# Seven half products for the first pair too, neighbouring chunks' products joined, and another order of the list

## The chip, the cores and the metric

The kernel runs on one core of one Trainium2 chip. Its time is the device time of one launch in microseconds; the profile is of one execution and splits it by engine: PE multiplies matrices (PEld loads its weights), DVE, ACT and POOL work elementwise, SP issues most DMAs. All data are float32.

## The reference

A gated recurrence over the sequence per head, with a complex gate, and then a low-rank mixer. Batch 4, heads 8, sequence 768, head size 48, so the model width is 384 and the mixer's inner width 1536.

```python
def _attn_ref(q, k, v, a_re, a_im):
    mag = np.sqrt(a_re * a_re + a_im * a_im)
    scale = np.minimum(mag, 0.999) / (mag + 1e-06)
    a_re_n, a_im_n = (a_re * scale, a_im * scale)
    ...
    for t in range(S):
        ar, ai = (a_re_n[:, :, t, :, None], a_im_n[:, :, t, :, None])
        new_re = ar * S_re - ai * S_im
        new_im = ar * S_im + ai * S_re
        kv = np.einsum('bhd,bhe->bhde', k[:, :, t], v[:, :, t])
        S_re, S_im = (new_re + kv, new_im)
        y[:, :, t] = np.einsum('bhd,bhde->bhe', q[:, :, t], S_re)

def _moe_ref(x, U, V, w_ch1, w_ch2):
    xt = x.transpose(0, 2, 1)
    h = xt @ U @ V
    u = x + h.transpose(0, 2, 1)
    ch = np.maximum(u @ w_ch1, 0.0) @ w_ch2
    return (u + ch).astype(np.float32)
```

`U` is 768x32, `V` 32x768, `w_ch1` 384x1536 (called w1 below), `w_ch2` 1536x384 (w2).

## The kernel before

**Chunks and pairs.** The sequence is cut into chunks of 128 positions, 6 in a batch and 24 in all, i = 0 to 23. A chunk is worked on in halves of 64. Two neighbouring chunks make a pair of the mixer, m = 0 to 11, three pairs in a batch.

**A chunk.** The gates' logarithms and angles are summed along the sequence by products with a triangle (L777, L782, L842); ACT makes exponentials (es) and sines and cosines (cs) of them, for which it loads another table each time (L463). The running angle is handed from one chunk group to the next by a carry: one small DMA on POOL's queue (L828) from the tile F into the next gate tile, which DVE reads at L836 and L837 before PE can form the next prefix (L842). DVE multiplies q and k by es and cs (L469), and the result is turned, by PE for the first six chunks and by a transposing DMA after that.

`chain(i)` then records the products of a chunk. `products` (L956) are keys by queries, with the array split 112x64; DVE masks them into AT (`copy_predicated`, L959). `state` (L976) is keys by values on tiles of 64x48, into two banks; DVE adds them to the running state (GM and G, L472, and G times its decay T, L469). `inside` (L1005) is AT by values on 64x64 and `before` (L1013) the state by queries on 112x64, both into the same two banks y, which ACT copies into xo, the attention's output (L1022, L1024). A matmul in float32 is two records in the trace.

**The mixer.** For a batch, `rank` (L1048) forms U-transposed by x; ACT copies it to r (L1054); `spread` (L1071) multiplies it by V, and DVE adds that to xo (`mixed`), which is now u. `turned` (L1087) transposes u into uT. The first layer of pair 0 is made ahead of the mixing (`up`, L1102) and then corrected by V times the tile `more` (`corrected`, L1142, `more` copied by ACT at L1128); pair 1 takes `up` after the mixing; pairs 2 to 11 take `up_fewer` (L1214), fifteen block products. ACT and DVE apply the relu and sums into h, for pair 0 into the tile `extra`.

**The second layer.** Pair 0 takes `down(cc)` (L1303): 12 products of 128x384 for each of its two chunks, over w2 in steps of two blocks, so that each step needs only the part of w2 that it reads. Later pairs take `down_two()` (L1346): the pair's 2x2 block product by seven half products, each six matmuls of 128x192, of sums of h's blocks (`sums`, DVE L1338) and differences of w2's blocks (`w2s`, made once by DVE at L652 from the whole of w2, in the tile `stage`). The first pair that uses it also turns one quarter of w2 into a difference in place (L1416). DVE adds the results onto xo (L472), and `leave` sends them out. w1 and w2 come from memory in pieces through `stage`, and ACT and DVE split each piece into a high and a low part (L466, L616, L620, L624, L472) during the first 120 us.

**What sets the order.** Every step is recorded with its engine, what it reads, writes and takes over, and ORDER is the list of record numbers in which the steps are issued, for all engines; each engine runs its share in that order, so an instruction that waits holds all behind it on its engine. SPARE and WARM put idle matmuls of the identity (fillers, L1506 and L1513) ahead of the record numbers that they name; SPARE counts matmuls of 128 columns, WARM lists column counts in units of 128. Of PSUM, five banks go round among the prefix, state, output and transpose steps, two hold the mixer's results (`up`, `few`, `down`), one the keys by queries.

## Time and profile before

| | us |
|---|---|
| median of 3 runs (lowest, highest) | 530.83 (529.35, 532.6) |
| profiled execution | 529.77 |
| its span | 528.0 |
| first matmul starts after | 7.7 |
| PE busy | 509.3 (6670 records) |
| DVE busy | 414.5 |
| ACT busy | 346.0 |
| POOL busy | 31.6 |

A line of the profile names an engine, the line of the kernel, the operation and the tiles out<-in by the program's names without buffer numbers, with a shape of partitions x elements. In a timeline it begins with the start and the duration in us; in a group `x` is the number of records, followed by total us and mean ns, and by the idle time of the engine just ahead of them. `[2.10 <-ACT more L1128]` is idle time of the engine ahead of an instruction, and what ended it.

### The profile page before, as it was taken

How to read it: one execution, taken by the hardware profiler on the slowest of the kernel's cores; microseconds unless marked ns; L12 is line 12 of the kernel's file. 1: busy time of each engine (PE TensorE's matmuls, PEld its weight loads, DVE VectorE, ACT ScalarE, POOL GpSimd, SP SyncE). 2: the span in 40 equal slices, each digit the busy share in tenths (PEclk: the TensorE clock that was granted, in tenths of full speed). 3: DMA queues.
4: the chain of work that ended last, by engine and by line, in shares of the span. 5: the costliest groups of instructions: out<-in, count | busy, mean ns of one | idle time of the engine just before them, and what ended most of it. 6: DMA issues, size and time to landing. Idle time of an engine off the chain costs nothing.

```text
span 528.0 us, 15692 instructions
## 1 busy us (share of the span) xinstructions
PE 509.3 (96%) x6670; PEld 460.3 (87%) x6670; DVE 414.5 (79%) x787; ACT 346.0 (66%) x555; POOL 31.6 (6%) x61
## 2 busy tenths in 40 slices
PE   4999999899999999999999999999999999999996
PEld 2777887666998997999999989999999989999996
DVE  4779897799989987898798797878796575958452
ACT  8899998998869978978896768843543313131100
POOL 1000000001010000101011000110000000000110
PEclk9999999999999999999999999999999999999998
DMA  9959958479999998999899958999897543333101
GB/s 226 173 115 270 209 115 191 140 138 217 197 215 244 216 215 145 204 217 202 205 198 227 210 144 175 170 242 229 192 217 178 108 90 61 76 60 61 39 32 35
DMA packets 280670, 87.06 MB, mean 165 GB/s; under 512 B 271288, under 2 KB 272784, under 8 KB 280592
## 3 DMA queue, kind: packets, MB, share of 16 engines
q1 hardware_dynamic: 278384, 81.63, 76.0%
q0 software_dynamic: 2208, 4.35, 2.4%
q8 instruction: 54, 0.88, 0.7%
q14 instruction: 24, 0.20, 0.1%
HBM read 43.03 MB, written 23.63 MB: 126 GB/s over the span
## 4 chain that ended last, share of the span: by engine, by line
PE 88%; ACT 5%; DMA 3%; DVE 2%; issue 1%; SPq 0%; ACTq 0%
PE down L1346 25%; PE few L1214 14%; PE bank L1214 11%; PE up L1102 6%; PE inner L956 4%; PE bank L1013 4%; PE bank L976 4%; PE down L1303 3%; PE bank L1005 2%; DMA gate<-F 2%; PE bank L1071 2%; PE bank L1087 2%; ACT gate L466 1%; PE bank L777 1%; PE bank L782 1%; PE bank L842 1%
## 5 line engine op out<-in xcount | busy, mean ns | idle before, releaser
L466 ACT ACTIVATE gate<-gate 128x768 f32<-128x768 f32 (+2 forms) x85 | 86.1, 1018 | 25.8 <-DMA gate<-in_a_im_dram 14.7
L1346 PE MATMUL down<-w,h 128*128 128x192 f32 x396 | 70.4, 328 | 0.0
L466 ACT ACTIVATE QK<-QKC 128x768 uint16<-128x768 uint16 (+1 forms) x72 | 58.5, 848 | 13.1 <-DVE QKC L469 7.9
L1346 PEld LDWEIGHTS down<-w,h 128*128 128x128 f32 x396 | 64.6, 190 | 1.2 <-issue 0.8
L469 DVE TENSOR_TENSOR QKC<-qk,cs 128x768 f32<-128x768 f32 x48 | 44.9, 952 | 1.0 <-ACT cs L466 0.6
L472 DVE TENSOR_TENSOR xo<-down,xo 128x192 f32<-128x192 f32 (+1 forms) x79 | 29.9, 385 | 14.3 <-PE down L1346 14.1
L1222 ACT COPY h<-few 128x512 f32<-128x512 f32 x35 | 20.2, 583 | 27.8 <-PE few L1214 27.6
L1222 ACT COPY h<-bank 128x512 f32<-128x512 f32 x25 | 14.3, 588 | 36.0 <-PE bank L1214 31.0
L1346 PE MATMUL down<-stage 128*128 128x192 f32 x198 | 37.2, 328 | 0.0
L1102 PE MATMUL up<-uT,w 128*128 128x256 f32 x144 | 33.8, 383 | 0.0
L1346 PEld LDWEIGHTS down<-stage 128*128 128x128 f32 x198 | 32.5, 190 | 0.3 <-issue 0.2
L1102 PEld LDWEIGHTS up<-uT,w 128*128 128x128 f32 x144 | 26.7, 190 | 4.9 <-issue 0.6
L1290 POOL DMA_DIRECT2D out_dram<-xo x32 | 18.5, 590 | 202.9 <-DVE xo L472 164.5
L463 ACT ACT_TABLE_LOAD x22 | 28.2, 1283 | 1.1 <-PEq L1567 0.7
L828 POOL DMA_DIRECT2D gate<-F x15 | 12.0, 797 | 274.7 <-DVE stage L616 86.3
L1226 DVE CUSTOM_DVE_ANT_1 h<-few,h 128x512 f32<-128x512 f32 x31 | 21.0, 686 | 8.8 <-PE few L1214 8.1
L1214 PE MATMUL few<-extra,w 128*128 128x128 f32 x216 | 27.8, 275 | 0.0
L956 PE MATMUL inner<-QK 112*64 112x64 f32 x768 | 27.5, 224 | 0.2 <-DVE AT L959 0.2
L466 ACT ACTIVATE cs<-F 128x384 f32<-128x384 f32 x48 | 24.4, 518 | 3.9 <-DVE F L851 3.7
L956 PEld LDWEIGHTS inner<-QK 112*64 112x64 f32 x768 | 24.5, 138 | 2.4 <-issue 0.8
L1214 PEld LDWEIGHTS few<-extra,w 128*128 128x128 f32 x216 | 26.3, 192 | 0.1
L466 ACT ACTIVATE es<-bank 128x384 f32<-128x384 f32 x44 | 18.4, 502 | 9.2 <-PE bank L777 8.2
(185 smaller groups left out, 1166.8 us busy)
## 6 DMA issues: line engine op xcount, KB each, us to landing
xd<-QK SPq DMA_DIRECT2D x36, 512.0 KB
gate<-in_a_re_dram SPq DMA_DIRECT2D x48, 192.0 KB
gate<-in_a_im_dram SPq DMA_DIRECT2D x48, 192.0 KB
stage<-in_moe_w_ch_dram SPq DMA_DIRECT2D x12, 768.0 KB
qk<-in_q_dram SPq DMA_DIRECT2D x24, 192.0 KB
qk<-in_k_dram SPq DMA_DIRECT2D x24, 192.0 KB
VP<-in_v_dram SPq DMA_DIRECT2D x24, 192.0 KB
out_dram<-xo POOLq DMA_DIRECT2D x12, 192.0 KB, 4.2
```

Of the source, the lines that this page charges most:

```text
L463: ACT(1.37, rank, lambda: nc.scalar.preload_act_table_set(name), writes=[TABLE])
L466: return nc.scalar.activation(out=o, in_=i, func=f, **kw)
L469: nc.vector.tensor_tensor(out=o, in0=a, in1=b, op=OP.mult)
L472: nc.vector.tensor_tensor(out=o, in0=a, in1=b, op=OP.add)
L956: nc.tensor.matmul(out=get(*ps0)[r:r + HC, h], lhsT=k_of(h, r, HC), rhs=q_of(h, r, HC), start=True, stop=True, tile_position=(0, r))
L976: nc.tensor.matmul(out=get(*dk[r])[x:x + D, h], lhsT=get(*ks)[at, h, x // DP, 0:D], rhs=get(*VPi)[at, h], start=True, stop=True, tile_posi ...
L1013: nc.tensor.matmul(out=get(*y[u])[side(r, u), p], lhsT=q_of(h, r * HC, HC), rhs=get(*(mid_G if r else ("G", i - 1)))[:, h], start=False, s ...
L1102: nc.tensor.matmul(out=get(*ps)[:, e], lhsT=w1[:, f, (ff + e) * 128:(ff + e + 1) * 128], rhs=get(*uT)[:, f], start=(f == 0), stop=(f == KD ...
L1214: nc.tensor.matmul(out=get(*ps)[:, q], lhsT=w()[:, q * 128:(q + 1) * 128], rhs=v[0](), start=(n == 0 and q == 0), stop=True, skip_group_ch ...
L1222: ACT(c_act(n3 * CH) - 0.045, RU, lambda i=i, k=k: nc.scalar.copy(out=at(i, k), in_=get(*ps)), [ps], [o])
L1226: DVE(c_dve(n3 * CH), RU, lambda i=i, k=k: nc.vector._custom_dve(dve_ops.TENSOR_ADD_SAT, out=at(i, k), in0=get(*ps), in1=at(i, k), s0=math ...
L1346: nc.tensor.matmul(out=get(*to)[:, part], lhsT=x(j), rhs=y[:, j], start=(first and j == 0), stop=(j == KH - 1), skip_group_check=not first)
```

## The change

PLAIN goes from 1 to 0: pair 0 too takes `down_two()`. Its h is the tile `extra`; the turning of w2's quarter (L1416, after the change L1459) moves to pair 0, which now needs all of w2 and its differences. JOIN = 8: from chunk 8 on, where a chunk is not the first of its batch, its `state` products and its predecessor's `inside` are recorded as one step (`fused_x`), and its predecessor's two `before` and its own `products` as another (`fused_y`); the addition into G and the multiplication by T, the masking and the predecessor's copies to xo follow the second. These are 14 of the 24 chunks. The spread no longer names uT among what it reads; the transposes take uT over instead. ORDER, SPARE and WARM are replaced by others. Below L1040 the lines shift by 43, above it by a few: L1102 becomes L1145, L1142 L1185, L1087 L1130, L1048 L1091, L1071 L1114, L1346 L1389, L1338 L1381, L1506 L1549, L1513 L1556; L956 becomes L962, L976 L974, L1005 L998, L1013 L1006.

```diff
--- before.py
+++ after.py
@@ -29,101 +29,100 @@
 ORDER = (
...
-    5, 97, 96, 0, 1, 2, 3, 102, 99, 101, 103, 4, 104, 105, 106, 107, 98, 116, 100, 115, 117, 118, 119, 10, 154, 8, 111, 112, 16, 9, 230, 108, 231,
...
+    5, 96, 0, 1, 2, 3, 4, 99, 97, 102, 101, 103, 104, 105, 8, 98, 116, 100, 115, 117, 9, 111, 106, 107, 108, 109, 118, 119, 120, 121, 125, 126, 122,
...
 SPARE = {
-    410: 3, 447: 1,
+    413: 3, 416: 6, 430: 4, 462: 1,
 }
...
 WARM = {
-    112: (2, 1), 126: (1,), 136: (2, 2, 2, 2, 2, 2, 1), 141: (2,), 162: (2, 2, 2), 235: (2, 2, 2, 2, 1), 242: (2,), 245: (2,), 259: (2, 2, 1), 266: (1, 1, 1, 1, 1, 1, 1, 1, 1),
+    125: (4,), 136: (4, 2, 2, 2, 2, 1), 141: (2,), 162: (2, 2, 2), 187: (1,), 235: (2, 2, 2, 2, 2, 2, 2), 242: (3,), 245: (2,), 259: (1,), 266: (2, 2, 2, 2, 1),
 }
...
@@ -352,7 +351,7 @@
     KH = KF // 2
     DH = DM // 2
 
-    PLAIN = 1
+    PLAIN = 0
     NS = 5
     FEWER, SINGLE, AHEAD = 2, 3, 1
     NCH = S // CH
@@ -369,6 +368,7 @@
     PARTS = [[(n, n + 1) for n in range(GC)]] + [[g] for g in GROUPS[1:]]
     NG = len(GROUPS)
     AGAIN = range(NG)
+    JOIN = 8
 
     EARLY, SPREAD = 6, (0, 1, 2)
     SPLIT = range(3, NG)
@@ -948,51 +948,44 @@
             return get(*QK)[0:DQ, 1, h * CH + lo:h * CH + lo + n]
 
         ps0 = ("inner", i)
-        psum(ps0, "A", [128, H, HC])
+        last = c == NCH - 1
+        joined, joins = c > 0 and i >= JOIN, not last and i + 1 >= JOIN
+        G, mid_G = ("G", i), ("GM", i)
+        ks, dk = ("qkc", 2 * i + 1), [("dk", (i, r)) for r in range(2)]
+        parts_k = range(1 if last else 2)
+        y, xi = [("y", (i, r)) for r in range(2)], ("xo", i)
+        y_in = [VPi, ATi, mid_G] + ([("G", i - 1)] if c else [])
 
         def products():
             for h in range(H):
                 for r in range(0, CH, HC):
                     nc.tensor.matmul(out=get(*ps0)[r:r + HC, h], lhsT=k_of(h, r, HC), rhs=q_of(h, r, HC), start=True, stop=True,
                                      tile_position=(0, r))
-        PE(0.947, RL, products, [QK], [ps0], takes=[ATi], way=1, steps=4 * H)
-        DVE(0.17 + 0.00104 * H * HC, RL, lambda: nc.vector.copy_predicated(
-            out=get(*ATi), mask=mask.bitcast(I32).unsqueeze(1).to_broadcast([128, H, HC]), data=get(*ps0)), [ps0, ("mask", 0)], [ATi])
-
-        G, mid_G, last = ("G", i), ("GM", i), c == NCH - 1
-        ks, dk = ("qkc", 2 * i + 1), [("dk", (i, r)) for r in range(2)]
-        buffer(mid_G, "GM", 2, [DQ, H, D])
-        if not last:
-            buffer(G, "G", 2, [DQ, H, D])
-        parts_k = range(1 if last else 2)
-        for r in parts_k:
-            psum(dk[r], "Y", [128, H, D], [128, H, DP])
-
-        def state(h0):
-            for h in range(h0, h0 + HH):
+
+        def kept():
+            DVE(0.17 + 0.00104 * H * HC, RL, lambda: nc.vector.copy_predicated(
+                out=get(*ATi), mask=mask.bitcast(I32).unsqueeze(1).to_broadcast([128, H, HC]), data=get(*ps0)), [ps0, ("mask", 0)], [ATi])
+
+        def state(h0, n=HH):
+            for h in range(h0, h0 + n):
                 for r in parts_k:
                     at = slice(r * HC, (r + 1) * HC)
                     for x in (0, DP):
                         nc.tensor.matmul(out=get(*dk[r])[x:x + D, h], lhsT=get(*ks)[at, h, x // DP, 0:D], rhs=get(*VPi)[at, h],
                                          start=True, stop=True, tile_position=(r * HC, x))
-        for h0 in (0, HH):
-            PE(0.443, RR, lambda h0=h0: state(h0), [ks, VPi], [dk[r] + (h0,) for r in parts_k], way=3,
-               steps=4 * HH * len(parts_k),
-               takes=[mid_G] + ([] if last else [G]))
 
         half0, half1 = (lambda r=r: get(*dk[r])[0:DQ] for r in range(2))
-        if c:
-            DVE(c_dve(DM), RR, lambda: add(get(*mid_G), get("G", i - 1), half0()), [("G", i - 1), dk[0]], [mid_G])
-        else:
-            ACT(c_act(DM), RR, lambda: nc.scalar.copy(out=get(*mid_G), in_=half0()), [dk[0]], [mid_G])
-        if not last:
-            DVE(c_dve(DM), RR, lambda: add(get(*G), get(*mid_G), half1()), [mid_G, dk[1]], [G])
-            DVE(c_dve(DM), RR, lambda: mul(get(*G), get(*G), T_of(i)), [("T", group_of(i))], [G])
-
-        y, xi = [("y", (i, r)) for r in range(2)], ("xo", i)
-        for r in range(2):
-            psum(y[r], "Y", [128, HH, D], [128, HH, CH])
-        buffer(xi, "xo", 8, [128, DM])
+
+        def states(first):
+            if not first:
+                pass
+            elif c:
+                DVE(c_dve(DM), RR, lambda: add(get(*mid_G), get("G", i - 1), half0()), [("G", i - 1), dk[0]], [mid_G])
+            else:
+                ACT(c_act(DM), RR, lambda: nc.scalar.copy(out=get(*mid_G), in_=half0()), [dk[0]], [mid_G])
+            if not last and first != joined:
+                DVE(c_dve(DM), RR, lambda: add(get(*G), get(*mid_G), half1()), [mid_G, dk[1]], [G])
+                DVE(c_dve(DM), RR, lambda: mul(get(*G), get(*G), T_of(i)), [("T", group_of(i))], [G])
 
         def side(r, u):
             return slice((r ^ u) * HC, (r ^ u) * HC + HC)
@@ -1013,18 +1006,68 @@
                     nc.tensor.matmul(out=get(*y[u])[side(r, u), p], lhsT=q_of(h, r * HC, HC),
                                      rhs=get(*(mid_G if r else ("G", i - 1)))[:, h], start=False, stop=True,
                                      tile_position=(0, (r ^ u) * HC), skip_group_check=True)
-        PE(0.44, RR, inside, [VPi, ATi, mid_G] + ([("G", i - 1)] if c else []), y, way=3, takes=[xi], steps=4 * H)
+
+        def befores():
+            for r in range(0 if c else 1, 2):
+                before(r)
+
+        def rooms():
+            for r in range(2):
+                psum(y[r], "Y", [128, HH, D], [128, HH, CH])
+            buffer(xi, "xo", 8, [128, DM])
+
+        def halves(a):
+            return a.rearrange("p (a u d) -> p a u d", u=2, d=D)
+
+        def leaves():
+            ACT(c_act(HH * D) - 0.04, RR, lambda: nc.scalar.copy(out=halves(get(*xi))[:, :, 0], in_=get(*y[0])), [y[0]], [xi + (0,)])
+            for r in range(2):
+                ACT(c_act(HH * D) + 0.04, RR, lambda r=r: nc.scalar.copy(out=halves(get(*xi))[r * HC:(r + 1) * HC, :, 1],
+                                                                         in_=get(*y[1])[side(r, 1)]), [y[1] + (r,)], [xi + (r + 1,)])
+        b_in = [QK, mid_G] + ([("G", i - 1)] if c else [])
+        psum(ps0, "A", [128, H, HC])
+        buffer(mid_G, "GM", 2, [DQ, H, D])
+        if not last:
+            buffer(G, "G", 2, [DQ, H, D])
+        for r in parts_k:
+            psum(dk[r], "Y", [128, H, D], [128, H, DP])
+        if joined:
+            p_inside, p_in, p_y, p_befores, p_b, p_leaves, p_rooms, p_takes = pending.pop(i - 1)
+            p_rooms()
+
+            def fused_x():
+                state(0, H)
+                p_inside()
+            PE(1.3, RR, fused_x, [ks, VPi] + p_in, [dk[r] for r in parts_k] + p_y, way=3, steps=4 * H * len(parts_k) + 4 * H,
+               takes=[mid_G] + p_takes)
+            states(True)
+
+            def fused_y():
+                p_befores()
+                products()
+            PE(1.8, RR, fused_y, p_b + [QK], p_y + [ps0], takes=[ATi], way=1, steps=8 * H)
+            states(False)
+            kept()
+            p_leaves()
+        else:
+            PE(0.947, RL, products, [QK], [ps0], takes=[ATi], way=1, steps=4 * H)
+            kept()
+            for h0 in (0, HH):
+                PE(0.443, RR, lambda h0=h0: state(h0), [ks, VPi], [dk[r] + (h0,) for r in parts_k], way=3,
+                   steps=4 * HH * len(parts_k),
+                   takes=[mid_G] + ([] if last else [G]))
+            states(True)
+        if joins:
+            pending[i] = inside, y_in, y, befores, b_in, leaves, rooms, [xi]
+            return
+        rooms()
+        PE(0.44, RR, inside, y_in, y, way=3, takes=[xi], steps=4 * H)
         if c:
             PE(0.467, RR, lambda: before(0), [QK, ("G", i - 1)], [y[0] + (0,), y[1] + (0,)], way=1, steps=2 * H)
         PE(0.467, RR, lambda: before(1), [QK, mid_G], [y[0] + (1,), y[1] + (1,)], way=1, steps=2 * H)
-        def halves(a):
-            return a.rearrange("p (a u d) -> p a u d", u=2, d=D)
-        ACT(c_act(HH * D) - 0.04, RR, lambda: nc.scalar.copy(out=halves(get(*xi))[:, :, 0], in_=get(*y[0])), [y[0]], [xi + (0,)])
-        for r in range(2):
-            ACT(c_act(HH * D) + 0.04, RR, lambda r=r: nc.scalar.copy(out=halves(get(*xi))[r * HC:(r + 1) * HC, :, 1],
-                                                                     in_=get(*y[1])[side(r, 1)]), [y[1] + (r,)], [xi + (r + 1,)])
-
-
+        leaves()
+
+    pending = {}
 
     def mixer(m, ahead=False):
         i0 = m * MC
@@ -1070,7 +1113,7 @@
                         at, c = slice(cc * MC * R, (cc + 1) * MC * R), c0 + cc
                         nc.tensor.matmul(out=get(*ps[cc])[:, y * DH:(y + 1) * DH], lhsT=V[at, c * CH:(c + 1) * CH],
                                          rhs=get(*r)[at, y * DH:(y + 1) * DH], start=True, stop=True, tile_position=(cc * MC * R, 0))
-            PE(0.76, R0, products, [r, ("V", 0)] + [uT + ("kept",)] * (m >= AHEAD), ps, way=5, steps=8)
+            PE(0.76, R0, products, [r, ("V", 0)], ps, way=5, steps=8)
             return ps
 
         def mixed(cc, ps):
@@ -1085,7 +1128,7 @@
             def turn():
                 for f in range(KD):
                     nc.tensor.transpose(out=get(*tr)[:, f], in_=get(*u)[:, f * 128:(f + 1) * 128], identity=ident)
-            PE(0.33, R0, turn, [u], [tr], steps=KD)
+            PE(0.33, R0, turn, [u], [tr], takes=[uT], steps=KD)
             to = lambda: get(*uT)[:, :, cc * CH:(cc + 1) * CH]
             if cc or m >= 3:
                 ACT(c_act(DM) - 0.045, R0, lambda: nc.scalar.copy(out=to(), in_=get(*tr)), [tr], [uT + (cc,)])

```

In the new list PE has 42 matmuls of 128x192 more in the second layer and none of the 24 of 128x384; 14 fillers by SPARE in place of 4, and 52 units of 128 columns by WARM in place of 55. In what follows, rows of the order stand as line, operation, out<-in with tile or buffer names, shape, and how many in a row.

PE around pair 0's first layer, before (`up` is its result, `more` its correction, `ident` a filler or a transpose, w_76 is w1):

```order
L1142 MATMUL up<-V,more 128x256 x2
L1506 MATMUL up<-ident 128x128
L1102 MATMUL up<-uT,w_76 128x256 x6
L1087 MATMUL bank_63<-ident,xo 128x128 x3
L1506 MATMUL up<-ident 128x128 x3
L1142 MATMUL up<-V,more 128x256 x2
```

The same place after:

```order
L1185 MATMUL up<-V,more 128x256 x2
L1549 MATMUL up<-ident 128x128 x3
L1185 MATMUL up<-V,more 128x256 x4
L1549 MATMUL up<-ident 128x128 x6
L1185 MATMUL up<-V,more 128x256 x2
L1549 MATMUL up<-ident 128x128
L1145 MATMUL up<-uT,w_76 128x256 x12
```

The corrections now stand together with ten fillers among them, and twelve `up` matmuls follow in place of six. PE at the start of pair 0's second layer, before (w_77 is w2, `extra` is h):

```order
L976 MATMUL bank_64<-VP_117,QKC_105 48x48 x2
L976 MATMUL bank_65<-VP_117,QKC_105 48x48 x2
L1303 MATMUL down<-w_77,extra 128x384 x6
L842 MATMUL bank_61<-GS_96,prefix_r 128x384
L842 MATMUL bank_61<-GS_97,prefix_r 128x384
L1303 MATMUL down<-w_77,extra 128x384 x14
```

And after:

```order
L1130 MATMUL bank_61<-ident,xo 128x128 x3
L1130 MATMUL bank_62<-ident,xo 128x128 x3
L1549 MATMUL down<-ident 128x128 x4
L1389 MATMUL down<-w_77,extra 128x192 x12
L1389 MATMUL down<-stage,extra 128x192 x6
L1389 MATMUL down<-stage 128x192 x9
L1389 MATMUL down<-stage,more 128x192 x3
```

The transposes of pair 1 and four fillers now stand ahead of the first half product, and the products read `stage` and `more`, where the differences and sums lie. DVE around the differences of w2, before:

```order
L469 TENSOR_TENSOR QKC_107<-qk,cs 128x16x48
L469 TENSOR_TENSOR QKC_103<-qk,cs 128x16x48
L652 TENSOR_TENSOR stage<-w_77 128x1152
L469 TENSOR_TENSOR qk<-qk,es 128x768
L836 CAST GS_96<-gate 128x384
L837 TENSOR_TENSOR GS_97<-gate,GS_96 128x384
L652 TENSOR_TENSOR stage<-w_77,stage 128x1152
L472 TENSOR_TENSOR xo<-down,xo 128x384
L736 ISA gate<-gate 128x768
```

And after:

```order
L472 ISA w_77<-w_77,stage 128x1536
L652 TENSOR_TENSOR stage<-w_77 128x1152
L836 CAST GS_96<-gate 128x384
L837 TENSOR_TENSOR GS_97<-gate,GS_96 128x384
L652 TENSOR_TENSOR stage<-w_77,stage 128x1152
L851 SCALAR_TENSOR_TENSOR F<-F,bank_65 128x384
L652 TENSOR_TENSOR stage<-w_77,stage 128x1152
L469 TENSOR_TENSOR QKC_107<-qk,cs 128x16x48
L1381 TENSOR_TENSOR stage<-extra 128x384 x2
L1459 TENSOR_TENSOR w_77<-w_77 128x6x192
```

The differences are made at one go right behind the last low part of w2, and pair 0's sums and the turned quarter follow; before, those of pair 0 didn't exist, and an xo step of 128x384 stood among the differences.

171 rows, old and new, of the table ORDER are left out of this document.

## The prediction

> **What bounds the kernel now.** I read the page first, for the engine that is busy to the end; then PE's waits, for what it still waits for; then busy time by stretches, for the engine that is next in line.
>
> From the page: busy time by engine, the granted clock in 40 slices of 13.2 us, and the chain that ended last.
>
> ```profile
> PE 509.3 (96%) x6670; PEld 460.3 (87%) x6670; DVE 414.5 (79%) x787; ACT 346.0 (66%) x555; POOL 31.6 (6%) x61
> PEclk9999999999999999999999999999999999999998
> PE 88%; ACT 5%; DMA 3%; DVE 2%; issue 1%; SPq 0%; ACTq 0%
> ```
>
> PE sets the end: it is busy for 96% of the span at full clock and carries 88% of the chain. So a change counts by the matmul time it removes and by the waits of PE it makes or ends. PE's waits, with total, number and longest in us:
>
> ```profile
> PE bank L782 <- DVE GL L742: 7.7, 1, 7.7
> PE up L1142 <- ACT more L1128: 2.1, 1, 2.1
> PE down L1346 <- DVE xo L472: 1.1, 1, 1.1
> PE down L1346 <- DVE stage L1338: 0.7, 1, 0.7
> PE bank L1071 <- ACT r L1054: 0.6, 1, 0.6
> ```
>
> The 7.7 is the first matmul's. Only 4.5 us of waits remain behind it, so no reordering can win more than about that without removing matmuls. Busy time by stretches (span, then PE, PEld, DVE, ACT, POOL, clock, DMA share, GB/s) around the change:
>
> ```profile
> 110.00:120.00 10.00, 10.00 (x103) 6.88 (x102) 8.90 (x19) 8.68 (x14) 0.77 (x1) 1.00 0.54 125
> 120.00:140.00 20.00, 20.00 (x139) 14.52 (x138) 19.37 (x29) 16.93 (x21) 1.35 (x2) 1.00 0.99 227
> 140.00:160.00 20.00, 18.89 (x259) 17.59 (x258) 18.13 (x35) 15.77 (x26) 2.69 (x4) 1.00 0.93 196
> ```
>
> From 110 to 140 PE never stops, yet DVE is at 28.3 of 30: it is the engine that any added work there can turn into a bound.
>
> **Second layer of pair 0.** Before, it is 24 matmuls of 128x384, which the trace records as 48; a later pair is 42 matmuls of 128x192, recorded as 84. From the chain (start, duration):
>
> ```profile
> 118.86 9.03 PE down L1303 x28
> 385.00 13.65 PE down L1346 x84
> ```
>
> 28 records in 9.03 are 0.3225 each, so 48 are 15.5; the half products take 13.65: **-1.8**. It is certain up to a switch or two, being PE's own time.
>
> **Joins.** Matmuls of unlike array split cost extra where they meet. The same 32 records of a chunk's products, first with a change of split behind them, then without:
>
> ```profile
> 335.35 1.08 PE inner L956 x32
> 346.73 0.95 PE inner L956 x32
> ```
>
> The difference is 0.13. Counting such meetings in the two orders gives 155 before and 147 after: the 14 joins save fewer places than their number, because the old order had often put like products side by side. 8 x 0.13 = **-1.0**, between 0 (if waits take it) and -14 x 0.13 = -1.8 (if each join saves one).
>
> Joining also makes a chunk's state products wait for the masked copy of its predecessor, and postpones the predecessor's copies. The order puts other matmuls (half products, `few`) between these steps, and the rows above hold no wait of PE for such a copy, so I take 0; the third rival is that this fails.
>
> **Carries.** A carry is a 1.5 KB transfer on POOL's queue; DVE's reader L836 stands in program order and holds everything behind it. From the chain, L828's issues, and DVE's timeline:
>
> ```profile
> 151.00 6.34 DMA gate<-F
> 275.81 6.09 DMA gate<-F
> DMA to landing us min/median/max: 1.9/3.9/6.3
> 157.37 0.36 DVE L836 CAST GS<-gate 128x384 fp32r<-128x384 f32 x1 [1.59 <-DMA gate<-F]
> ```
>
> The two longest delayed DVE, and behind it PE's half products: the 1.1 and the 0.7 in PE's waits. Before, six of the 15 readers follow their issue with less than 1 us of DVE work between in the order; after, two do, with 2.6 and 3.6 us of PE work between. I take **-1.7** of the 1.8, bounds -1.8 and 0.
>
> The Trainium skill, "DMA: Bandwidth & Descriptors", section "Anatomy of one DMA — SWDGE (gpsimd) path", fits a DMA of this path as about 2.0 us plus bytes over 436 GB/s, some 2.0 for a carry; by it no reader would wait long and this term would be 0. The trace's 6.34 speaks against it.
>
> **Pair 0 starts later.** The seven products read differences of the whole w2 (L652) and sums of h (L1338), so they cannot start piece by piece as L1303 did at 114.37. What ACT and DVE do before that, and what PE has instead:
>
> ```profile
> 88.85 0.46 ACT L1054 COPY r<-rank 128x384 f32<-128x384 f32 x1
> 116.68 1.06 ACT L466 ACTIVATE stage<-stage 128x768 uint16<-128x768 uint32 x1
> 91.78 1.10 ACT L466 ACTIVATE stage<-stage 128x768 uint16<-128x768 uint32 x1 [2.04 <-DVE w L472]
> 118.21 0.95 DVE L472 CUSTOM_DVE_ANT_0 w<-w,stage 128x1536 uint16<-128x1536 uint16 x1
> L652 DVE TENSOR_TENSOR stage<-w,stage 128x1152 f32<-128x1152 f32 x2 | 2.7, 1351 | 0.0
> 157.76 0.56 DVE L837 TENSOR_TENSOR GS<-gate,GS 128x384 fp32r<-128x384 f32 x1
> L469 DVE TENSOR_TENSOR QKC<-qk,cs 128x768 f32<-128x768 f32 x48 | 44.9, 952 | 1.0 <-ACT cs L466 0.6
> 114.37 4.14 PE L1303 MATMUL down<-w,extra 128*128 128x384 f32 x12
> L1102 PE MATMUL up<-uT,w 128*128 128x256 f32 x144 | 33.8, 383 | 0.0
> 210.92 0.82 PE L1087 MATMUL bank<-ident,xo 128*128 128x128 f32 x6
> 210.46 0.62 PE L842 MATMUL bank<-GS,prefix_r 128*128 128x384 f32 x2
> 111.53 0.83 PE L1506 MATMUL up<-ident 128*128 128x128 f32 x6
> ```
>
> ACT goes from r at 88.85 to the last w2 conversion's end at 117.74, 28.9 us, of which at least 2.0 stand idle. The new order keeps about the same list between them, without some copies of QK (25 us by the durations of its forms); starting at r it ends between 112.4 and 116.7. I take 112.4, since r itself comes some 1.4 earlier: three up matmuls (6 records at 33.8 / 144 us, L1102 above) fall behind the rank products. Then DVE: 0.95 for the low part, 3 x 1.35 for the differences, 0.36 + 0.56 + 0.95 and an F step of about 0.55 between them, and the first sum: 8 us, so the products could start at 120.4.
>
> PE meanwhile has six more up matmuls (12 records x 33.8 / 144 = 2.8), three transposes (0.82 / 2 = 0.4) and two prefix products (0.62) ahead: 114.4 + 3.8 = 118.2. The ten fillers more are 10 x 0.28 = 2.8 at most; ten of the fourteen stand around the corrections L1142, where PE had waited 2.1 anyhow, and four just ahead of the half products, in the gap. The gap is **+2.2**; 0 if ACT is 2 us sooner, +4 to +6 if r comes when it did and ACT ends at 116.7.
>
> **Within pair 0's products.** Sums and xo steps are now in DVE's row between the products' quarters, with DVE nearly full. A pair's sums made PE wait 0.7 once (L1338 above): **+0.7**, bounds 0 and +2.
>
> DVE's own addition is:
>
> ```profile
> L1338 DVE TENSOR_TENSOR stage<-h 128x384 f32<-128x384 f32 x22 | 12.1, 552 | 0.3 <-ACT h L466 0.2
> L472 DVE TENSOR_TENSOR xo<-down,xo 128x192 f32<-128x192 f32 x66 | 22.8, 353 | 12.9 <-PE down L1346 12.9
> ```
>
> 8 x 0.552 + 6 x 0.353 less one 128x384 step of 0.552 = 6.0 us. I cost it at nothing beyond the 0.7: PE works from 118 to 140 without a stop, and DVE's steps for later chunks can slip behind it. If that cover is gone, it is the second rival.
>
> **End of chunk 11.** Before, 64 records of chunk 12's states stand between chunk 11's last products and the rank products; now none. The chunk 17 boundary of before shows what they hide:
>
> ```profile
> 204.14 0.64 PE L1013 MATMUL bank<-G,QK 112*64 112x48 f32 x16
> 205.49 0.31 ACT L1024 COPY xo<-bank 64x192 f32<-64x192 f32 x1
> 206.22 2.14 PE L1048 MATMUL bank<-xo,UV 128*32 128x384 f32 x24
> 209.91 1.49 DVE L472 TENSOR_TENSOR xo<-bank,xo 128x384 f32<-128x384 f32 x3 [0.33 <-PE bank L1071]
> ```
>
> The last product ends at 204.78, the last copy at 205.80: 1.0 us bare if nothing lies between. The transposes that now follow the spread directly wait for its addition on DVE (1.49 / 3 = 0.5): **+1.5**, bounds +0.7 (part covered by PE's delay) and +3 (an exponential of 1.5 us ahead of the copies on ACT).
>
> The dropped dependence of the spread (L1071) on kept uT, and the retuned start fillers (52 against 55 units of 128 columns, inside PE's start waits) I cost at 0.
>
> **Sum:** -1.8 - 1.0 - 1.7 + 2.2 + 0.7 + 1.5 = -0.1 on the profiled execution (span 528.0, itself 529.77 with 1.77 around it; the median of the runs, 530.83, is 1.06 above it). Applied to the median: **530.7**.
>
> **Rivals.**
> 1. Faster: the gaps are covered. With 0 at pair 0, 0 within it and +0.7 at chunk 11 the sum is -1.8 - 1.0 - 1.8 + 0.7 = -3.9; with the 1.8 of joins and also the r wait of 0.6 gone, -5.3: 525.5 to 526.9, say 526. For it: the gap of 2.2 is the difference of two estimates of about 120. Against: w2's conversions run through ACT at 8.68 of 10.
> 2. Slower: DVE becomes the bound. From 110 to 160 it has 50 - 46.4 = 3.6 us free and gets 6.0. If its delayed steps (sums of the next pairs, block sums for `few`, masked copies) come due for PE before 160, the 6.0 show whole: 530.7 + 6 = 537. It decides once DVE has less than about half a microsecond free between 115 and 160. Against: 3.6 are free there, and the stretch after 160 has slack to catch up.
> 3. The joins do nothing, because DVE's wait for the masked copy now stops PE at each of 14 places by as much as the 0.13 saved: 530.7 + 1.0 = 531.7.
> 4. The clock drops: a gap of more than 3 us at pair 0 (ACT's late end, +5) costs speed afterwards. For it nothing in this trace: the clock stays at 9 through the 2.1 us wait. Price: the gap of 5 instead of 2.2 and some 2 us of half speed losing 1 to 2: 535.
> The Trainium skill, "TensorE: Matmul & The Clock Gate", section "Part 1: The HAM clock gate", has the array fall to half clock after an idle window of about 3.4 us; no run here shows it yet.
>
> **Chances.** Forecast 0.47, rival 1 0.23, rival 2 0.15, rival 3 0.08, rival 4 0.07. About 1% is what a measurement of this kernel tells from no change: 525.5 and 536.1. Faster: 0.18, namely 0.13 of rival 1 and 0.05 of the forecast's low end (all bounds favourable). Slower: 0.17, namely 0.11 of rival 2, 0.03 of rival 4 and 0.03 of the forecast with the +6 gap. Same: 0.65. The range, 525.2 to 536.5, runs from rival 1's far end to just short of rival 2's.
>
> **What would show it.** Second layer: one block of 84 records in about 13.7 at pair 0. Start: PE idle 1 to 3 us, less its four fillers, ahead of the first L1389, its releaser a difference L652 or a sum L1381. Carries: no wait of DVE for gate<-F over 1 us. Chunk 11: PE waits for L1025 and for uT. Joins: fewer microseconds per record in L962 and L974. DVE in 120 to 160 above 39 of 40 would be rival 2. The forecast is wrong if PE's waits from 88 to 165 total under 3 us or over 9 us with the fillers counted (before: 3.2 of waits and 1.3 of fillers).

## The result and the profile after

| us | before | after |
|---|---|---|
| median of 14 runs each | 530.29 (529.35 to 532.6) | 536.81 (532.74 to 539.9) |
| profiled execution, its span | 529.77, 528.0 | 538.0, 536.2 |

The ratio is 1.0123, interval 1.010 to 1.0145: slower by about 6.5 us, and from lowest to highest spread over 7.2 us in place of 3.3. From the page of the kernel after: busy time, the granted clock in 40 slices of 13.4 us, the chain that ended last.

```profile
PE 512.5 (96%) x6714; PEld 466.0 (87%) x6714; DVE 419.0 (78%) x800; ACT 348.7 (65%) x555; POOL 32.2 (6%) x62
PEclk9999998999999999999999999999999999999999
PE 76%; DVE 11%; ACT 8%; issue 2%; DMA 1%; SPq 0%; DVEq 0%; ACTq 0%
```

PE still sets the end, but the seventh slice has lost clock, and the chain runs through DVE and ACT more. PE's waits of the kernel after:

```profile
PE bank L782 <- DVE GL L742: 8.0, 1, 8.0
PE bank L1114 <- ACT r L1097: 2.0, 1, 2.0
PE up L1549 <- DVE extra L1191: 1.7, 3, 0.8
PE bank L998 <- issue: 1.5, 1, 1.5
PE bank L974 <- issue: 1.1, 1, 1.1
PE bank L1006 <- issue: 1.1, 1, 1.1
PE inner L962 <- issue: 0.5, 1, 0.5
...
PE down L1389 <- issue: 0.4, 1, 0.4
```

The two carry waits of before are gone and r costs 2.0 in place of 0.6. New is 4.6 us of "issue", in which PE waits for nothing that the profile shows. Before, one wait of that kind had 0.4:

```profile
PE bank L976 <- issue: 0.4, 1, 0.4
```

Two of the places, from the timeline of PE after:

```profile
81.56 0.92 PE L974 MATMUL bank<-VP,QKC 64*48 64x48 f32 x31
83.54 0.20 PE L974 MATMUL bank<-VP,QKC 64*48 64x48 f32 x1 [1.07 <-issue]
...
86.29 0.68 PE L998 MATMUL bank<-VP,AT 64*64 64x48 f32 x31
88.47 0.25 PE L998 MATMUL bank<-VP,AT 64*64 64x48 f32 x1 [1.51 <-issue]
```

PE stops in the middle of a step, one record from its end: no tile can be what it waits for. Busy time by stretches (as in the prediction), before first, then after:

```profile
80.00:90.00 10.00, 10.00 (x246) 7.29 (x235) 7.51 (x13) 9.58 (x18) 0.76 (x1) 1.00 0.83 178
90.00:100.00 10.00, 7.90 (x68) 5.08 (x68) 6.96 (x14) 7.26 (x8) 0.20 (x1) 1.00 0.79 216
```

```profile
80.00:90.00 10.00, 7.32 (x236) 6.49 (x226) 6.97 (x12) 7.98 (x14) 0.00 (x0) 0.94 0.60 179
90.00:100.00 10.00, 10.00 (x80) 6.18 (x81) 7.21 (x14) 7.99 (x13) 0.96 (x1) 0.89 0.39 91
```

After has 0.94 and 0.89 of the clock here: 0.06 x 10 + 0.11 x 10 = 1.7 us of work lost, one stretch of 3.4 us at half clock from 88.8 on, right behind the two stops.

**What the stops are.** PE's queue for instructions stands among the DMA queues of the page (queue, kind: packets, MB, share):

```profile
q8 instruction: 54, 0.88, 0.7%
```

It has 54 packets of 16 KB (884,736 / 54 = 16,384 bytes), and PE issues 6714 matmuls and as many weight loads: 13,428 / 54 = 249 per packet. A stop is here a place where PE stands inside a step with no releaser but "issue". Counted from the start, the five longest of these stops come before the 1463rd, 2227th, 2482nd, 7066th and 10126th of PE's matmuls and weight loads. The distances are 764, 255, 4584 and 3060, which is 3, 1, 18 and 12 times 254.7 to 255: one block of 256, less an instruction or two of another kind in each. Each stop ends 1.2 to 1.6 us behind the end of the packet that loads the block. The stop of before (204.80 to 205.44, in front of the 5536th) is one of these too. So PE runs out of instructions where it uses up a block of short steps before the next has landed.

The traces bear this out beyond the five. Take the 442 blocks that PE enters after 40 us in the nine profiles of the table below. In 46 of them PE uses up the block before the packet of the next one has ended, or less than 1.2 us after. All 33 stops of a third of a microsecond or more stand at these 46; 31 stand at the end of a block that PE used up in under 5 us (96 blocks are that short).

The Trainium skill, "Runtime: NRT & Kernel Launch", section "Instruction fetch mechanics", describes such blocks of 16 KB or 256 instructions, fetched while the one before runs, and calls the cost of crossing into the next mostly hidden. By the traces here it is hidden in most blocks (409 of the 442), and 0.3 to 3.6 us where it isn't.

### The profile page after: what moved, and what is told of

Read it like the earlier page. It is cut to its first block, busy times and chain, and to the rows that moved or that the text cites. A ratio compares the mean times of both kernels' runs of the same rounds, so it can differ in the third digit from the quotient of the medians.

```text
span 536.2 us, 15791 instructions
## 1 busy us (share of the span) xinstructions
PE 512.5 (96%) x6714; PEld 466.0 (87%) x6714; DVE 419.0 (78%) x800; ACT 348.7 (65%) x555; POOL 32.2 (6%) x62
## 4 chain that ended last, share of the span: by engine, by line
PE 76%; DVE 11%; ACT 8%; issue 2%; DMA 1%; SPq 0%; DVEq 0%; ACTq 0%
PE down L1389 26%; PE few L1257 13%; PE bank L1257 11%; PE up L1145 4%; PE bank L1006 4%; PE inner L962 3%; PE bank L974 3%; ACT gate L466 2%; DVE QKC L469 2%; PE bank L998 2%; PE bank L1130 2%; PE bank L1114 1%; DVE xo L472 1%; PE bank L782 1%; PE bank L842 1%
## 5 line engine op out<-in xcount | busy, mean ns | idle before, releaser
L1389 PE MATMUL down<-w,h 128*128 128x192 f32 x396 | 70.8, 329 | 0.0
L466 ACT ACTIVATE QK<-QKC 128x768 uint16<-128x768 uint16 (+1 forms) x72 | 58.7, 850 | 11.6 <-DVE QKC L469 10.8
L1389 PEld LDWEIGHTS down<-w,h 128*128 128x128 f32 x396 | 64.6, 190 | 0.8 <-issue 0.2
L472 DVE TENSOR_TENSOR xo<-down,xo 128x192 f32<-128x192 f32 (+1 forms) x84 | 31.8, 383 | 23.3 <-PE down L1389 23.2
L1389 PE MATMUL down<-stage 128*128 128x192 f32 x216 | 40.5, 329 | 0.4 <-issue 0.4
L1389 PEld LDWEIGHTS down<-stage 128*128 128x128 f32 x216 | 35.4, 190 | 1.8 <-issue 0.7
L1145 PE MATMUL up<-uT,w 128*128 128x256 f32 x144 | 34.2, 385 | 0.0
L1145 PEld LDWEIGHTS up<-uT,w 128*128 128x128 f32 x144 | 26.6, 190 | 5.5 <-issue 0.8
L1333 POOL DMA_DIRECT2D out_dram<-xo x33 | 19.8, 634 | 191.0 <-DVE xo L472 147.7
L962 PE MATMUL inner<-QK 112*64 112x64 f32 x768 | 27.3, 224 | 0.8 <-issue 0.5
L962 PEld LDWEIGHTS inner<-QK 112*64 112x64 f32 x768 | 24.6, 138 | 3.1 <-issue 1.7
L974 PEld LDWEIGHTS bank<-VP,QKC 64*48 64x48 f32 x1408 | 19.5, 121 | 5.7 <-issue 3.1
```

The source lines that it names most:

```text
L466: return nc.scalar.activation(out=o, in_=i, func=f, **kw)
L472: nc.vector.tensor_tensor(out=o, in0=a, in1=b, op=OP.add)
L962: nc.tensor.matmul(out=get(*ps0)[r:r + HC, h], lhsT=k_of(h, r, HC), rhs=q_of(h, r, HC), start=True, stop=True, tile_position=(0, r))
L974: nc.tensor.matmul(out=get(*dk[r])[x:x + D, h], lhsT=get(*ks)[at, h, x // DP, 0:D], rhs=get(*VPi)[at, h], start=True, stop=True, tile_posi ...
L1145: nc.tensor.matmul(out=get(*ps)[:, e], lhsT=w1[:, f, (ff + e) * 128:(ff + e + 1) * 128], rhs=get(*uT)[:, f], start=(f == 0), stop=(f == KD ...
L1333: queue.dma_start(out=out[b, c * CH:(c + 1) * CH, lo:hi], in_=get("xo", i)[:, lo:hi])
```

## The experiments

Theory A: stops at block boundaries, and the half-clocked stretches behind them, are the loss; so its size hangs on where in the program the boundaries fall. Theory B: the loss lies in waits for data that the new order makes.

**Moving the boundaries.** n fillers ahead of the first matmul, where PE waits 7.7 to 8.0 us for DVE, add 4n instructions (a matmul in float32 is two records, each with its weight load) and move each later boundary by as many; the order of the work stays. The kernels with 8x8 fillers (after by 64, 128, 192; before by 64, 128):

```diff
 WARM = {
+    111: (0,) * 16,
...
     def warm(u):
...
+        if u == 0:
+            nc.tensor.matmul(out=spare[0][0:8, 0, 0:8], lhsT=ident[:, 0:8], rhs=ident[:, 0:8], start=True, stop=True)
+            return
```

The first four had them 128x8 (`out=spare[0][:, 0, 0:8], lhsT=ident`).

> The changed kernel with 25 narrow fillers (128x8) ahead of its first matmul, where PE is idle anyway: 100 more PE instructions, so that every later boundary of 256 instructions falls 100 instructions earlier in the program; nothing else moves. Theory A (PE's instructions come in blocks of 256, 16 KB each on queue q8, and PE stops where a block of short matmuls is used up faster than the next one lands): the boundaries fall into the densest runs (five blocks that take under 3 us against none before the shift), stops inside a step at other places, 538 to 542 us. Theory B (the loss sits in data waits that the new order makes: h, r, pair 0): the time stays at 536.8 within 1.5, the waits at the same instructions.

> The same with 44 narrow fillers, 176 instructions. Theory A: the phase with the fewest blocks under 3.5 us, stops of 1 us or more fall from four to two or fewer, 531 to 535 us. Theory B: 536.8 within 1.5.

> The kernel before with 28 narrow fillers ahead of its first matmul, 112 instructions. Theory A: the kernel before runs without such stops only because its boundaries fall well; moved by 112 they fall into the dense runs, two or more stops of about 1 us, 533 to 537 us. Theory B: 530.3 within 1.

> The kernel before with 8 narrow fillers, 32 instructions, a phase with no block under 3.7 us. Theory A: no stops, 529.5 to 531 us. Theory B: 530.3 within 1.

The 128x8 fillers took 0.43 us each (25 in 10.84), so that with 25, 44 and 28 of them PE's first product started 4.1, 12.2 and 5.6 us late. If this lateness counts in full, 540.52, 551.56 and 543.29 us are 536.4, 539.4 and 537.7 without it; theory A had 538 to 542, 531 to 535 and 533 to 537, so its count of blocks missed all three. With 8 fillers PE started on time, and the kernel before, shifted by 32, took 534.23 (ratio 1.0048, 1.0018 to 1.0078), where theory A's count of blocks had expected none or a gain. The time does hang on the place of the boundaries, but the number of short blocks alone doesn't say where they hurt. The 8x8 fillers that follow take 0.06 us each (16 in 0.95).

> The changed kernel with 16 tiny fillers (8x8) ahead of its first matmul, 64 PE instructions, meant to end before PE's first matmul was due. Theory A (stops at block boundaries): the stops lie at other instructions than in the changed kernel but again 140 to 185 past a multiple of 256 in the count of matmuls and weight loads, ending 1.2 to 1.5 us behind a packet on q8; the time differs from 536.8 by 1 us or more, either way. Theory B (data waits): 536.8 within 1, waits at the same instructions.

> The same with 32 tiny fillers, 128 instructions. Theory A: as for 64, and the medians of the shifts of 0, 64, 128 and 192 lie 3 us or more apart, the lowest under 535. Theory B: all four within 1.5 us of 536.8.

> The same with 48 tiny fillers, 192 instructions; expectations as for 128.

> The kernel before with 16 tiny fillers (8x8) ahead of its first matmul, 64 instructions. If the changed kernel's loss is its denser list, the kernel before keeps its 530 to 534 at other block places too, and stays 3 us or more below the changed kernel at the same shift (538.2). If the kernel before was only lucky in the place of its blocks, it comes to 535 to 538 here and at 128.

> The same with 32 tiny fillers, 128 instructions; the changed kernel has 534.6 at this shift. Denser list: 530 to 533. Luck of the place: 535 or more.

First products started at 7.6 to 8.2 us in all of these. Stops are summed from the starts of PE's matmuls and weight loads (gaps over 0.3 us behind 40 us, at a boundary, from one start to the next); half clock is the time for which the profile shows a granted clock of 0.5, up to PE's end, so half of it is lost.

| kernel, shift | runs | median us (lowest to highest) | profiled execution | its stops | its half clock |
|---|---|---|---|---|---|
| before, 0 | 14 | 530.29 (529.35 to 532.6) | 529.77 | 0.6 | 0 |
| before, 32 | 10 | 534.23 (530.47 to 538.17) | 538.17 | 6.5 | 10.2 |
| before, 64 | 4 | 538.66 (537.22 to 540.67) | 538.79 | 7.7 | 13.7 |
| before, 128 | 4 | 539.68 (537.96 to 542.69) | 537.96 | 9.7 | 3.4 |
| after, 0 | 14 | 536.81 (532.74 to 539.9) | 538.0 | 6.1 | 3.4 |
| after, 0, on another chip | 4 | 539.76 (537.74 to 541.66) | 540.89 | 7.1 | 10.2 |
| after, 64 | 4 | 538.21 (537.56 to 539.84) | 538.86 | 3.2 | 6.8 |
| after, 128 | 10 | 534.61 (531.64 to 536.93) | 534.4 | 2.7 | 3.4 |
| after, 192 | 4 | 539.53 (538.08 to 541.76) | 540.29 | 7.0 | 6.8 |

Moving nothing but boundaries makes the kernel before slower by 9 us, with an interval of 1.0153 to 1.0231 for the ratio at 128. For the kernel after the spread is 5 us, of which 3 show up between two chips without any shift. The profiled execution of before at 32 is the longest of its ten runs, so its stops are more than that kernel's median has. Not all of the half clock stands behind stops: in the profiles of before at 32, after at 64 and after at 128, 6.8, 3.4 and 3.4 us of it follow waits for data (for `more`, `extra` and r). The kernel before at 64, PE's waits:

```profile
PE bank L783 <- DVE GL L743: 5.2, 1, 5.2
PE bank L1014 <- issue: 3.4, 2, 2.9
PE bank L977 <- issue: 3.4, 1, 3.4
```

It now has what the kernel after has, and more. So theory B falls for most of the loss, and so does the thought that the new list is merely denser: at equal shifts the two kernels stand at 538.7 against 538.2 and 539.7 against 534.6. Over the shifts of 0, 64 and 128 the medians average 536.2 before and 536.5 after; three places, on more than one chip, are few for such an average. The kernel before was fast because of the place at which its boundaries fell, and the change moved them.

That the added fillers themselves cost the time is unlikely: after with 32 of them (ratio to the kernel before beside it 1.0075, 1.0047 to 1.0103) is faster than after with none (1.0123, 1.010 to 1.0145). A shift by a whole block, which would leave the boundaries in place, was not run.

**Taking the density away at two stops.** In the kernel after, 640 matmuls and weight loads in a row between 78 and 90 us belong to short steps of chunks 4 and 5. Two first-layer steps are moved in between them (one neighbour in the list moves along):

```diff
 ORDER, the entries around the moved ones
-    ... 295, ... 296, ... 391, 390, ... 297, 372, 67, 393, ...
+    ... 295, 391, 390, ... 372, 67, 296, 297, 393, ...
```

> The changed kernel unaltered, beside the next three on one chip: 535 to 539 us with stops at the blocks that begin near the 1463rd, 2227th and 2482nd of PE's matmuls and weight loads.

> The changed kernel with two first-layer steps of pair 0 (6 records of 128x256 each, 1.3 us) moved later in the list, one in front of chunk 5's states, one in front of its inner products, into the run of 640 matmuls and weight loads that holds nothing but short steps of chunks 4 and 5. PE's work is the same. Theory A (a block of short matmuls runs out before the next lands): the stops at 82 and 87 us shrink by 1.5 to 3 us together, the half-clocked stretch behind them goes in most runs, 2 to 4 us faster than the run beside it. Theory B (data waits): no change within 1 us, or slower by the hole that the steps leave behind.

The unaltered kernel beside it took 539.76 (537.74 to 541.66), the loosened one 537.16 (535.68 to 538.86). With four runs each the ranges overlap, so the 2.6 us are likely and not certain; the profiles say more. Stretches of the unaltered kernel's profile, then of the loosened one's:

```profile
80.00:90.00 10.00, 6.95 (x199) 6.13 (x191) 6.96 (x12) 7.89 (x14) 0.00 (x0) 0.79 0.71 191
90.00:100.00 10.00, 9.70 (x77) 5.94 (x78) 5.06 (x9) 5.46 (x9) 0.96 (x1) 0.70 0.12 24
```

```profile
80.00:90.00 10.00, 9.12 (x221) 7.74 (x217) 6.29 (x11) 7.19 (x13) 0.00 (x0) 1.00 0.63 166
90.00:100.00 10.00, 10.00 (x82) 5.58 (x80) 8.14 (x16) 9.20 (x13) 0.96 (x1) 1.00 0.42 107
```

The stop of 1.8 in front of the 2227th is gone, that in front of the 2482nd went from 1.95 to 1.10, and with them the clock stays up here. Stops that weren't touched remain, and one of 1.8 near 65 us has a half-clocked stretch of 3.4 us behind it. That is theory A's mechanism. This profile has a second stretch of 3.4 us, at 113.5, behind PE's waits for `extra`; it counts against the gain and isn't explained by theory A.

**The end of chunk 11.** The first of two kernels moves the copy of r ahead of the table load on ACT; the second also moves DVE's additions onto xo ahead of the QKC products on DVE that wait for cs:

```diff
-    920, 1182, 1199, 1198, 1207, 592, 921, 591, 922, ... 1212, 926, 923, ...
+    920, 921, 1182, 1199, 1198, 592, 591, 922, ... 926, 923, ... 1004, ... 1001, 1207, 1212, ...
```

> The changed kernel with one entry of the list moved: ACT copies r of chunks 6 to 11 right behind the rank products, ahead of the table load and the two steps of cs. PE's instructions and their blocks are unchanged. Theory A: the wait of PE for r falls from 2.0 to about 0.7 us, its gap from 2.5 to 1.1, the time by 1.0 to 1.5 us and no more, stops stay. Theory B (the new waits for data are most of the loss, this the longest of them): over 2.5 us, since the end of the half-clocked stretches would go with it.

> The changed kernel with the list altered at the end of chunk 11: r copied right behind the rank products, and on DVE the four additions onto xo ahead of the two QKC products that wait for cs. No PE instruction moves. If DVE's wait for cs is what held the transposes in the run with r alone (3.4 us there), the gaps of 2.5 and 0.6 us fall to about 1.1 and 0.6, with about 1 us in front of chunk 12's states instead: 1 to 2 us faster than 536.8. Otherwise no gain.

PE's timeline with r first, then with both:

```profile
213.09 1.57 PE L1103 MATMUL bank<-r,V 64*128 64x192 f32 x16 [0.59 <-ACT r L1086]
217.75 1.48 PE L1119 MATMUL bank<-ident,xo 128*128 128x128 f32 x9 [3.10 <-DVE xo L461]
```

```profile
216.04 1.57 PE L1103 MATMUL bank<-r,V 64*128 64x192 f32 x16 [0.59 <-ACT r L1086]
217.69 1.48 PE L1119 MATMUL bank<-ident,xo 128*128 128x128 f32 x9
220.82 0.94 PE L963 MATMUL bank<-VP,QKC 64*48 64x48 f32 x64 [1.65 <-DVE QKC L458]
```

r comes 1.4 us sooner, and PE waits 3.1 for xo instead; with both, the wait stands at chunk 12's states. The two took 540.65 and 539.66 us, the unaltered kernel 536.81 and, on another chip, 539.76: no gain. DVE's wait for cs (4.7 us after, 6.1 with r first) is the limit there, whatever stands first.

**Fillers, and the first part undone.** One kernel makes SPARE's 14 fillers 8x8. Another gives pair 0 its 24 plain products at the places of the half products, and 18 tiny fillers so that later boundaries stay:

```diff
-            nc.tensor.matmul(out=to[:, 0:CH], lhsT=ident, rhs=ident, start=True, stop=True)
+            nc.tensor.matmul(out=to[0:8, 0:8], lhsT=ident[:, 0:8], rhs=ident[:, 0:8], start=True, stop=True)
```

```diff
-    PLAIN = 0
+    PLAIN = 1
...
+TINY = {422: 18}
```

> The changed kernel with its 14 fillers of SPARE made 8x8 in place of 128x128, as many instructions, so that no block boundary moves. They stand behind PE's waits for the relu of h, not inside them, so they cost PE their own 14 x 0.22 = 3.1 us. Theory A (the stops and the half clock are the loss; the data terms came out near the sum): 1.5 to 3 us faster, 534 to 535.5, unless PE then waits for the correction's tile more or w2's differences. Rival (the fillers keep the clock up or only fill a wait): same or slower than 536.8.

> The changed kernel with the first part undone: pair 0's second layer by 24 matmuls of 128x384 at the places of its half products, the turned quarter of w2 behind them, and 18 tiny fillers in front so that block boundaries behind it stay where they were. Theory A: 1.8 us of matmuls more and up to 1 us of tiny fillers, less nothing: 537.5 to 539.5. Rival (the seven products at pair 0 are what costs, by late differences of w2 or by DVE): 2 us or more faster than 536.8.

With tiny fillers it took 539.03 us, no gain. A stretch of its profile:

```profile
115.00:122.00 7.00, 6.01 (x28) 4.42 (x29) 6.73 (x11) 6.89 (x11) 0.77 (x1) 0.52 0.37 58
```

The clock fell to 0.52 where it had stayed at 1.00 with the full fillers (110 to 120 in the kernel after), and 7 x 0.48 = 3.4 us of work went. That is about what the 14 fillers take (14 x 0.28 = 3.9), so the rival, that they pay for themselves by the clock, fits. The combined kernel further down, with tiny fillers too, also lost the clock here for 6.8 us. But it isn't certain: three of the twelve profiles of the changed kernel and its variants with whole fillers lost it here as well, for 3.4 us each.

The kernel with plain products took 544.32, slower than either theory had it. Its 48 records went through in 15.2 us as forecast, but DVE waited 4.0 us for them and made the inputs of the next chunks' prefix late; PE waited 1.5 and 0.6 us for these, and the clock fell for 6.8 us behind that. The list isn't made for plain products, so this run doesn't price the first part; it only shows that taking the seven products back, in this list, doesn't bring the time back.

**Carries alone, in the kernel before.**

```diff
-    ... 757, ... 758, ... 511, ... 476, 480, ...      ... 1392, 1058, 1393, 1068, ... 1064, ...
+    ... 511, ... 476, 480, 757, 758, ...            ... 1058, 1068, ... 1064, 1392, 1393, ...
```

> The kernel before with two carry readers on DVE (those that waited 1.6 us at 157 and 1.7 at 282) moved behind three steps each that the second layer waits for; PE's instructions stay as they are. If the carry term of the prediction (-1.7) was right, PE's waits of 1.1 and 0.7 go: 1.0 to 1.8 us faster than the kernel before. Otherwise the wait comes back on ACT's gates: no gain.

531.11 us, ratio 1.0004 (0.998 to 1.0028): no gain. PE's waits then:

```profile
PE up L1131 <- ACT more L1117: 2.1, 1, 2.1
PE inner L945 <- DMA QK<-xd: 1.1, 1, 1.1
PE bank L1203 <- ACT xo L1013: 0.8, 1, 0.8
PE bank L1060 <- ACT r L1043: 0.6, 1, 0.6
```

The 1.1 and 0.7 behind the carries are gone, and a 1.1 and a 0.8 that weren't there have come, for a transposed QK and for an xo copy. The profiled execution, of 531.89 us, also ran at half clock for 3.4 us from 97.3 on, behind the wait of 2.1.

**Together.**

> The three together: 32 tiny fillers ahead of the first matmul (the shift of 128, 534.6 alone), tiny fillers by SPARE, r and the additions first. Theory A: the terms add, 534.6 - 2.2 - 1.5 = 531, at or slightly above the kernel before (530.6); with no stop and full clock 529. Theory B (data waits alone): 536.8 - 3.7 = 533 whatever the shift.

> The changed kernel with the shift of 128 and r and the additions first, its fillers whole: 534.6 less the gain of the boundary alone (0.5 to 1.5): 533 to 534, the clock nearer 1 than in the combined run, whose tiny fillers let it drop at 108 us.

With shift 128, r and additions first and tiny fillers, the kernel took 534.73 us (5 runs), where theory A had added up to 531. With whole fillers it took 534.99, where 533 to 534 was expected. The shift alone had 534.61. Nothing adds to it, and none of these beats the kernel before.

## Why the prediction was wrong

- **The step that failed** is the first: "a change counts by the matmul time it removes and by the waits of PE it makes or ends". It left out a third thing, which the trace of before held in one row that I passed over (0.4 us of "issue" at L976): PE's own instructions can come late. (Its 4.5 us of waits stopped at the rows down to 0.6; the whole list before has 1.4 us more.) The change adds 42 matmuls in front of some boundaries, takes 24 away and rewrites the list, so every boundary falls elsewhere. In the profile that cost 6.1 - 0.6 = 5.5 us of stops and 1.7 of clock, 7.2 of the 8.2 by which the spans differ. This sum takes each microsecond of stop and of lost clock for one of the span. The shifted kernels before say that this is too much: at 64 the profile has 7.1 us more of stops and 6.8 of lost clock, 13.9 together, and a span longer by 8.9; at 128 it is 10.8 against 8.2. So 7.2 is likely too much.
- **The rest of the sum** stood at -0.1 and is +1.0 (8.2 - 7.2), or more by as much as the stops count for less. So the terms came near to cancelling as forecast, though not each for its reason:
- *Second layer, -1.8:* right. The 84 records went from 126.31 to 140.58 with 0.65 of a prefix in between, 13.6 us, against 15.2 for the 48 of the run with plain products.
- *Joins, -1.0:* not to be seen, and open. The traces do have 155 and 147 changes of split, as the prediction counted; but the products of the chain (L962, L974, L998 and both forms of L1006) are busy for 96.3 us after and 94.4 before, with part of the clock's loss in the 96.3.
- *Carries, -1.7:* the waits went as forecast, and alone, in the kernel before, they are worth nothing. The term left out what is late next.
- *Pair 0 later, +2.2:* there was no gap. PE came to the first half product at 126.31, 8 us later than reckoned, some 6 of them by the stops and the clock (4.3 + 1.7). The differences of w2 came late as well: the last ended at 126.63 in place of about 120, and still before PE's first product that reads `stage`, where they lie, at 130.21. That there was no gap is luck, since both sides came late by about as much. What PE pays here is the fillers. The prediction had put them inside PE's waits for the relu of h; they stand behind these waits:

```profile
111.85 0.94 PE L1549 MATMUL up<-ident 128*128 128x128 f32 x6 [0.46 <-DVE extra L1191]
114.63 1.60 PE L1549 MATMUL up<-ident 128*128 128x128 f32 x12 [0.78 <-DVE extra L1191]
117.37 0.49 PE L1549 MATMUL up<-ident 128*128 128x128 f32 x2 [0.51 <-DVE extra L1191]
```

- *Within pair 0, +0.7:* there was none; PE ran through.
- *End of chunk 11, +1.5:* right in size, 1.4 for r and 0.3 for the transposes. The prediction called the rows that it took "chunk 17"; they were the boundary behind chunk 11 itself. Its reason was wrong, so the size is luck: it named late copies, and what came late was r, behind ACT's table load and cs, and the additions behind DVE's wait for cs.
- **Rival 2** (DVE full) came true in its sign and not in its effect: 39.2 us busy of 40 from 120 to 160, with PE at 20.00 of 20 in both halves.

```profile
120.00:140.00 20.00, 20.00 (x178) 18.53 (x177) 19.37 (x33) 16.75 (x22) 0.75 (x1) 1.00 0.92 199
140.00:160.00 20.00, 20.00 (x238) 18.44 (x237) 19.86 (x37) 16.04 (x27) 3.84 (x6) 1.00 0.90 211
```

- **Rival 4** (the clock drops) happened, behind stops of 1.3 and 1.7 us and not behind a gap at pair 0. The Trainium skill, "TensorE: Matmul & The Clock Gate", section "Part 1: The HAM clock gate", has half clock follow an idle window of about 3.4 us. The stretches here are 3.4 us long or multiples of it, but no single idle stretch in front of the one in the kernel after is: two stops of 1.3 and 1.7 us within 7 us were enough. PE's 2.1 us wait for `more` stands in six profiles of the kernel before and its variants: in two of them (shift 32 and the late carries) half clock follows it, in the other four it doesn't.

What stays open is why one packet is late and another isn't. Over the same 442 blocks, the packet starts 0.1 us (mean) behind PE's entry into the block before its own where the DMA engines are less than 30% busy within 2 us of that entry. It starts 1.3 us behind, in a tenth of the cases 3.2 or more, where they are over 95% busy; 21 of the 33 stops belong to these. That points to the queueing of the packet among the kernel's own transfers. No run here changed the transfers, so it isn't shown.

## What to carry to other kernels

Where a PE-bound kernel issues hundreds of short matmuls in a row, look for "issue" waits inside a step and count instructions: if they sit multiples of about 255 apart, the place of a boundary is part of the time, and two versions should be compared at several shifts (a few tiny fillers in an idle start) before a per cent is put down to anything else. Longer matmuls among the short ones give the next block time to land, as two of them did here. A wait that is taken away gains nothing if something else is late next: price that too.

## What the runs showed that was not expected

Tiny fillers ahead of the first matmul, in time in which PE idles, changed the same work by up to 9 us. Stops of 1 to 3.6 us in the supply of instructions then cost nearly as much again in clock, in the kernel before at 64. Fillers of 128 columns, at 0.28 us each, can be worth their time by keeping the clock: with 14 of them made tiny it stood at 0.52 for 7 us.
